# Two linear-attention blocks mixed by a gate: the gate weights issued ahead of the third chunk of key weights

## The chip, the cores and the metric

The kernel runs on one core of a Trainium2 chip. The metric is the device time of one execution in microseconds; a profiled execution also gives the span from its first to its last instruction.

## What is computed

The input `x` has 2048 rows of 640 numbers in bf16. Two linear-attention blocks A and B, of 32 heads with 20 numbers each, are applied to the same `x`, each with its own `wqkv` (640 x 1920) and `wo` (640 x 640), and a gate mixes them.

```python
def block(x, wqkv, wo):
    q, k, v = split_heads(x @ wqkv)                 # 32 heads of 20
    phi = lambda t: where(t > 0, t + 1, exp(t)) + 1e-6
    pq, pk = phi(q), phi(k)
    kv = einsum("bhsd,bhse->bhde", pk, v)
    z = einsum("bhsd->bhd", pk)
    o = einsum("bhqd,bhde->bhqe", pq, kv) / (einsum("bhqd,bhd->bhq", pq, z)[..., None] + 1e-6)
    return merge_heads(o) @ wo
g = sigmoid((x * gate_w).sum(-1, keepdims=True))
out = g * block(x, A_wqkv, A_wo) + (1 - g) * block(x, B_wqkv, B_wo)
```

The gate's sum costs no pass of its own: `gate_w` becomes one extra column (column 640) of B's key weights, so that the key matmuls of block B also give `x * gate_w` summed over each row.

## The kernel before

**Stages.** The rows of `x` are cut into 16 tiles of 128, and the 640 columns into five chunks of 128 (the contraction of the key and query matmuls). The stages on TensorE are: a few warm-up matmuls; the keys of all tiles for A and B (L660 and L661, and L825 where tiles are paired), with their phi on ScalarE and VectorE; the sums that stand for `kv` and `z` (L1186); the queries (L1058, L1154); products of weights (L1342, L1374, L1448); and the output matmuls (L1584), whose results are stored tile by tile.

**The planner.** Every operation is given to `op` or `dma` with an engine, an estimated cost, the buffers that it reads and writes, and other operations that it must follow (`after`). `Sched.run` then places operations one after the other at the earliest planned time of each engine. TensorE keeps the order in which its operations were given. The other engines take, of what could start, the operation with the earliest start, and among equals the one with the lowest `prio`, which is the order of giving unless stated otherwise. Between two operations of different engines the planner adds `HOP`, 60 ns. A load is planned with 450 ns of issue, 1500 ns of latency and its bytes at a given rate on one shared bus. `Sched.emit` writes the instructions in planned order, with a semaphore wait for each dependence that isn't known already.

**The first loads.** While the list `loading` isn't empty, `dma` chains the loads of one queue by `o.behind`, so that they are issued in the order in which they are given. ScalarE's queue gets three loads, L529 to L531: tile 1 of `x`; chunk 2 of A's key weights, through `ld_wk` with a planned size of 1280 bytes; and `gate_w`, as five rows of 128 numbers, into `GWZ`. SP's queue gets tile 0 of `x`, chunks 0, 1, 3 and 4 of A's key weights, the five chunks of B's, the transposing loads of later tiles (`xt_dma`), and the rest.

**What else ScalarE has at the start.** The operation `table` (L486) loads the table of activation functions and runs one small activation; its `prio` is 10**6, and it needs the constant `EPSC` that GpSimd sets (L484).

**What GpSimd does at the start.** It sets constants, clears `GWZ` (L502, the operation `zgw`), makes the identity `IDN` (L494), and sets a few pad columns. The load of the gate weights names `zgw` in `after`, since it fills five rows of a tile that must be zero elsewhere.

**What TensorE does at the start.** After the warm-up (L587), `x_tp` turns tiles 0 and 1 by matmuls with `IDN` (L600). VectorE copies tile 0, and ScalarE tile 1, into `XT` (L617). Then come the keys of A for both tiles, chunk by chunk. `gate_col` stands between chunk 3 and chunk 4: it turns `GWZ` by one matmul (L637), and VectorE copies the five columns into B's key weights (L640). The keys of B follow:

```python
    for c in range(4):
        for t in range(2):
            k_step("A", t, c, pss[t])
    gate_col()
    for c in range(4, NC):
        for t in range(2):
            k_step("A", t, c, pss[t])
```

Each `k_step` is a pair of matmuls, of 512 columns (L660) and of 128 (L661; 129 in block B with the gate's column). It waits for its chunk of key weights and for its part of `XT`.

Of the kernel before, what the change touches and what calls it, by code (L numbers as in the profile page):

```python
# [6 lines left out]
ACT = mybir.ActivationFunctionType  # L7
# [8 lines left out]
NC = 5  # L16
# [97 lines left out]
class Sched:  # L114
# [9 lines left out]
    def op(self, eng, fn, cost, ins=(), outs=(), after=(), prio=None, name="", dma=None):  # L124
        if eng == "ACT" and dma is None:
            after = list(after) + self.consts
        o = Op(eng, fn, cost, list(ins), list(outs), after, (self.base or len(self.ops)) if prio is None else prio, name, dma)
        self.ops.append(o)
        return o
# [184 lines left out]
def body(nc, A_x, A_wqkv, A_wo, B_x, B_wqkv, B_wo, gate_w, out, log=None):  # L314
# [24 lines left out]
    GWZ = sb("GWZ", [128, 128], bf)  # L339
# [105 lines left out]
    def dma(q, name, dst, src, nbytes, ins=(), outs=(), after=(), issue=450.0, transpose=False, prio=None, rate=330.0):  # L445
        timing = (rate, 1500.0 if loading else 1700.0) if not transpose else (140.0, 1500.0) if loading else (400.0, 1950.0)

        def fn(e):
            d = dst() if callable(dst) else dst
            with nc.allow_non_contiguous_dma(reason="layout"):  # L450
                return e.dma_start(d, src() if callable(src) else src, transpose=transpose)

        o = op(q, fn, 0.0, ins, outs, after, prio=prio, name=name, dma=(issue, nbytes) + timing)
        if loading:
            o.behind = chain.get(q)
            chain[q] = o
        return o
# [28 lines left out]
    def table(e):  # L486
# [12 lines left out]
        outs=[bid],  # L499
        name="idn",  # L500
    )
    zgw = op("POOL", lambda e: e.memset(GWZ[:, :], 0.0), 200.0, name="zgw")  # L502
# [4 lines left out]
    def ld_x(q, t):  # L507
        dma(q, "x%d" % t, XN[:, t, 0:D], x[128 * t : 128 * t + 128, :], 163840, outs=[bxn[t]])

    def ld_wk(q, X, c, size=163840):  # L510
        dma(q, "wk%s%d" % (X, c), WK[X][:, c, 0:D], wqkv[X][128 * c : 128 * c + 128, D : 2 * D], size, outs=[bwk[X, c]])
# [15 lines left out]

    bgw = Buf("gw5")
    ld_x("ACT", 1)  # L529
    ld_wk("ACT", "A", 2, 1280)  # L530
    dma("ACT", "gw", GWZ[0:NC, :], gate_w.rearrange("(c p) -> c p", p=128), 1280, outs=[bgw], after=[zgw])  # L531
    for c in range(NC):
        if c == 0:
            ld_x("SP", c)
# [1205 lines left out]
def bass_gated_mix__linear_attn_block__linear_attn_block__prompt_kernel(nc, *args):  # L1740
    body(nc, *args)
# [28 lines left out]
```

## Time and profile before

| What | us |
|---|---|
| Median of three runs | 174.75 |
| Lowest and highest of them | 174.69, 175.47 |
| The profiled execution | 174.98 |
| Its span | 173.6 |
| TensorE's matmuls busy | 171.0 |
| VectorE busy | 142.7 |
| ScalarE busy | 115.9 |

In the profile, PE is TensorE's matmuls, PEld its weight loads, DVE is VectorE, ACT is ScalarE, POOL is GpSimd and SP is SyncE. ACTq and SPq are the queues on which ScalarE and SP issue DMAs; an entry there is the time of the issue, not of the transfer. The brackets behind an entry give the idle time of the engine before it and what is taken to have ended that. Where a wait was for several things, the one named may have been done long before, and another, often a DMA, was the last. L451 is the line in `dma` that issues every load and store.

### The profile page before, as it was taken

To read this page: it belongs to the slowest core of one execution; us is meant where nothing else is said; L and a number is where in the kernel's file an instruction comes from. 1 tells how busy PE (TensorE), PEld (TensorE's weight loads), DVE (VectorE), ACT (ScalarE), POOL (GpSimd) and SP (SyncE) were. 2 spreads that over 40 slices of the span, in tenths; PEclk is the share of its full clock that TensorE was granted. 3 is DMA by queue.
4 is the path that set the end of the run, shared out by engine and by line. 5 is a ranking of instruction groups with operands and counts; after the bars stand their busy time and mean duration, and the time that the engine had idled before them with its cause. 6 is when DMAs were issued, how large, how long until landed. Compare 5 with 4: busy or idle time off the path is not lost.

```text
span 173.6 us, 3381 instructions
## 1 busy us (share of the span) xinstructions
PE 171.0 (99%) x1327; PEld 107.4 (62%) x1327; DVE 142.7 (82%) x262; ACT 115.9 (67%) x225; POOL 4.9 (3%) x17
## 2 busy tenths in 40 slices
PE   9999999999999999999999999999999999999995
PEld 4555555555577776666555565655556677777773
DVE  2277999999999946958889989799999993999541
ACT  5379999999953323235998895767799773556423
POOL 2000000000000070000000000000000000000000
DMA  7969999990000025339920003276860012370035
GB/s 231 296 133 116 230 369 365 358 180 7 4 0 0 0 42 99 75 66 184 230 58 0 4 2 73 66 203 160 261 182 17 0 38 79 82 230 4 0 112 190
DMA packets 33035, 20.59 MB, mean 119 GB/s; under 512 B 18260, under 2 KB 32892, under 8 KB 33020
## 3 DMA queue, kind: packets, MB, share of 16 engines
q1 hardware_dynamic: 31918, 19.59, 44.5%
q10 hardware_dynamic: 1102, 0.80, 1.6%
q8 instruction: 10, 0.16, 0.4%
q14 instruction: 5, 0.04, 0.1%
HBM read 10.88 MB, written 4.26 MB: 87 GB/s over the span
## 4 chain that ended last, share of the span: by engine, by line
PE 99%; ACT 0%; issue 0%; DVE 0%
PE ps L1186 22%; PE ps L1584 22%; PE ps L660 15%; PE ps L1058 14%; PE ps L1154 10%; PE ps L825 6%; PE ps L661 4%; PE ps L587 1%; PE ps L1448 1%; PE ps L1374 1%; PE ps L1342 1%; PE ps L600 1%; ACT PKS L1649 0%; DVE ONE L483 0%; PE ps L637 0%
## 5 line engine op out<-in xcount | busy, mean ns | idle before, releaser
L660 PE MATMUL ps<-WKW,XT 128*128 128x512 bf16 x120 | 34.0, 382 | 0.0
L661 PE MATMUL ps<-WKW,XT 128*128 128x128 bf16 (+1 forms) x120 | 26.4, 220 | 0.0
L1186 PE MATMUL ps<-TX,PKS 128*128 128x321 bf16 (+1 forms) x160 | 23.5, 300 | 0.0
L708 ACT ACTIVATE EKT<-ps 128x640 bf16<-128x640 f32 x30 | 20.8, 722 | 2.9 <-PE ps L661 2.5
L660 PEld LDWEIGHTS ps<-WKW,XT 128*128 128x128 bf16 x120 | 11.8, 98 | 14.5 <-DVE XT L617 0.5
L1186 PEld LDWEIGHTS ps<-TX,PKS 128*128 128x128 bf16 x160 | 15.6, 98 | 6.9 <-DVE DEN L1235 0.2
L1186 PE MATMUL ps<-XN,PKS 128*128 128x321 bf16 (+1 forms) x120 | 18.2, 300 | 0.0
L1186 PEld LDWEIGHTS ps<-XN,PKS 128*128 128x128 bf16 x120 | 11.7, 98 | 5.2
L897 DVE TENSOR_TENSOR PKS<-PKS 128x1280 bf16<-128x1280 bf16 (+2 forms) x20 | 13.0, 686 | 0.0
L720 ACT ACTIVATE PKS<-ps 128x640 bf16<-128x640 f32 x18 | 12.8, 724 | 0.0
L1216 ACT ACTIVATE EKT<-ps 128x321 f32<-128x321 f32 (+1 forms) x12 | 5.2, 438 | 11.2 <-PE ps L1186 5.6
L661 PEld LDWEIGHTS ps<-WKW,XT 128*128 128x128 bf16 x120 | 11.8, 98 | 0.0
L1090 ACT ACTIVATE EQ<-ps 128x512 bf16<-128x512 f32 x18 | 10.7, 604 | 1.5 <-PE ps L1058 1.0
L1165 ACT ACTIVATE EQ<-ps 128x1024 bf16<-128x1024 f32 x8 | 8.2, 1028 | 4.8 <-PE ps L1154 3.7
L711 DVE TENSOR_SCALAR EKT<-EKT 128x1280 bf16<-128x1280 bf16 (+1 forms) x20 | 8.3, 421 | 2.7 <-ACT EKT L708 2.7
L1058 PE MATMUL ps<-XT,WQA 128*128 128x512 bf16 x36 | 10.2, 379 | 0.0
L1067 ACT ACTIVATE PKS<-ps 128x512 f32<-128x512 f32 x12 | 7.0, 602 | 4.1 <-PE ps L1058 4.1
L1154 PE MATMUL ps<-XT,WQB 128*128 128x512 bf16 x40 | 9.4, 381 | 0.0
L1154 PE MATMUL ps<-XT,WQA 128*128 128x512 bf16 x40 | 9.3, 380 | 0.0
L1221 DVE TENSOR_TENSOR WKW<-ps,EKT 128x320 bf16<-128x320 f32 x12 | 5.8, 487 | 3.1 <-PE ps L1186 3.0
L726 DVE TENSOR_TENSOR PKS<-PKS,EKT 128x1280 bf16<-128x1280 bf16 x9 | 7.4, 820 | 0.1
L1607 DVE TENSOR_TENSOR PKS<-ps,EKT 128x320 bf16<-128x320 f32 x7 | 3.4, 492 | 4.7 <-PE ps L1584 2.2
(182 smaller groups left out, 339.3 us busy)
## 6 DMA issues: line engine op xcount, KB each, us to landing
out_dram<-PKS SPq DMA_DIRECT2D x15, 160.0 KB, 1.8
XN<-in_A_x_dram SPq DMA_DIRECT2D x1, 2240.0 KB, 9.3
WKW<-in_B_wqkv_dram SPq DMA_DIRECT2D x5, 160.0 KB, 3.7
WQA<-in_A_wqkv_dram SPq DMA_DIRECT2D x1, 800.0 KB, 10.9
WQB<-in_B_wqkv_dram SPq DMA_DIRECT2D x1, 800.0 KB, 12.1
WVA<-in_A_wqkv_dram SPq DMA_DIRECT2D x1, 800.0 KB, 11.9
PKS<-in_B_wqkv_dram SPq DMA_DIRECT2D x1, 800.0 KB, 5.1
PKS<-wpsA SPq DMA_DIRECT2D x1, 800.0 KB, 5.5
```

What stands on the lines that cost most here:

```text
L660: e.matmul(a[:, 0:512], l, WK[X][:, c, 0:512], start=(c == 0), stop=(c == NC - 1))
L661: return e.matmul(a[:, 512:w], l, WK[X][:, c, 512:w], start=(c == 0), stop=(c == NC - 1))
L708: op("ACT", lambda e, i=i, ps=ps: e.activation(evg(i), psg(ps), ACT.Exp), act_cost(D), ins=[ps] + first, outs=[ek, b], name="ke")
L711: lambda e: e.tensor_scalar(EK[:, ek.slot : ek.slot + n, :], EK[:, ek.slot : ek.slot + n, :], 1.0, EPS, op0=ALU.min, op1=ALU.add),
L720: op("ACT", lambda e, X=X, ps=ps: e.activation(pkt(X, t), psg(ps), ACT.Relu), act_cost(D), ins=[ps], outs=[rk], name="kr")
L825: r = e.matmul(a[:, lo:hi], l, m[:, lo:hi], start=(first and i == 0), stop=(i == len(prs) - 1), skip_group_check=not first)
L897: lambda e: e.tensor_tensor(out=out, in0=a, in1=b, op=ALU.subtract),
L1058: r = e.matmul(PS[:, ps.slot, :], w, x, start=(first and i == 0), stop=(i == len(prs) - 1), skip_group_check=not first)
L1090: o = [op("ACT", lambda e: e.activation(EQ[:, eq.slot + h, :], pv(), ACT.Exp), act_cost(512), ins=ins, outs=[eq, ex], name="qe")]
L1154: r = e.matmul(PS[:, ps.slot + h, :], WQ[X][:, c, g::5], XT[:, c, 1024 + 512 * h : 1536 + 512 * h], start=(c == 0), stop=(c == NC - 1))
L1186: r = e.matmul(PS[:, ps.slot, 0:w], reg[:, j, :], mov(j, w), start=(first and j == 0), stop=(j == 7), skip_group_check=not first)
L1584: r = e.matmul(PS[:, ps.slot, 0:HALF], reg(g), mov(g), start=(first and g == 0), stop=(g == NC - 1), skip_group_check=not first)
```

## The change

The load of the gate weights is given to ScalarE's queue ahead of chunk 2 of A's key weights, and no longer behind it. Nothing else in the file changes. Since the queue's loads are chained in the order of giving, chunk 2 is then issued behind the gate weights, and behind their wait for `zgw`.

```diff
@@ -527,8 +527,8 @@
 
     bgw = Buf("gw5")
     ld_x("ACT", 1)
+    dma("ACT", "gw", GWZ[0:NC, :], gate_w.rearrange("(c p) -> c p", p=128), 1280, outs=[bgw], after=[zgw])
     ld_wk("ACT", "A", 2, 1280)
-    dma("ACT", "gw", GWZ[0:NC, :], gate_w.rearrange("(c p) -> c p", p=128), 1280, outs=[bgw], after=[zgw])
     for c in range(NC):
         if c == 0:
             ld_x("SP", c)
```

## The prediction

> **What bounds the kernel now.** I read the page first, then the chain, then the first 7 us engine by engine, since the change touches only two DMA issues at the start. The page:
>
> ```profile
> span 173.6 us, 3381 instructions
> ...
> PE 171.0 (99%) x1327; PEld 107.4 (62%) x1327; DVE 142.7 (82%) x262; ACT 115.9 (67%) x225; POOL 4.9 (3%) x17
> ...
> PE 99%; ACT 0%; issue 0%; DVE 0%
> ```
>
> TensorE is busy from 0.3 us to the last stores, and the chain that ended last is PE work for 99%. So the only ways for this change to reach the end are a stall, or the closing of a hole, in TensorE's first stream. ScalarE's own order of time, from the timeline (start, duration, instruction):
>
> ```profile
> 0.12 0.40 ACTq L451 DMA_DIRECT2D XN<-in_A_x_dram  x1
> 0.56 0.44 ACTq L451 DMA_DIRECT2D WKW<-in_A_wqkv_dram  x1
> 1.04 0.57 ACTq L451 DMA_DIRECT2D GWZ<-in_gate_w_dram  x1
> 1.64 1.28 ACT L487 ACT_TABLE_LOAD   x1 [1.64 <-POOL XN L505]
> 2.94 0.20 ACT L488 ACTIVATE SCR<-EPSC 128x1 f32<-128x1 f32 x1
> 3.51 0.87 ACT L617 ACTIVATE XT<-ps 128x128 bf16<-128x128 f32 x3 [0.38 <-PE ps L600]
> ```
>
> The second and third line are the two that trade places. GWZ must be cleared before its DMA is issued (after=[zgw]); GpSimd does that here:
>
> ```profile
> 0.46 0.20 POOL L502 MEMSET GWZ<- 128x128 bf16 x1
> 0.69 0.29 POOL L494 TENSOR_SCALAR_AFFINE_SELECT IDN<-ONE 128x128 bf16<-128x128 bf16 x1
> ```
>
> The users are on PE's weight loads, from its timeline:
>
> ```profile
> 2.55 1.09 PEld L600 LDWEIGHTS ps<-IDN,XN 128*128 128x128 bf16 x10 [0.41 <-issue]
> 3.88 0.10 PEld L660 LDWEIGHTS ps<-WKW,XT 128*128 128x128 bf16 x1 [0.24 <-DVE XT L617]
> ...
> 5.25 0.10 PEld L660 LDWEIGHTS ps<-WKW,XT 128*128 128x128 bf16 x1
> ...
> 6.33 0.10 PEld L637 LDWEIGHTS ps<-IDN,GWZ 128*128 128x128 bf16 x1
> ```
>
> Counting the L660/L661 pairs (chunk by chunk, two tiles each), 3.88 is the first use of key chunk 0, 4.70 of chunk 1, 5.25 of chunk 2 (the load that moves), 5.79 of chunk 3, and 6.33 is the gate weights' only use. From 4.70 on, PE goes from pair to pair every 0.27 us with no idle entry: chunk 2 is not waited for now.
>
> When do loads land? One load at a time (time from issue to landing), first chunk 2 on ScalarE's queue, then chunk 3 on SP's:
>
> ```profile
> L451 ACTq DMA_DIRECT2D WKW<-in_A_wqkv_dram x1: 443/443/443, 0.6 to 0.6; - x1
> ...
> DMA to landing us min/median/max: 3.4/3.4/3.4
> ```
>
> ```profile
> L451 SPq DMA_DIRECT2D WKW<-in_A_wqkv_dram x1: 432/432/432, 1.4 to 1.4; - x1
> ...
> DMA to landing us min/median/max: 3.8/3.8/3.8
> ```
>
> So chunk 2 lands at 0.56 + 3.4 = 4.0, 1.25 us before its use. Read the same way, chunk 0 (issued 0.45) takes 3.3 and lands at 3.8, chunk 1 (0.91) takes 3.5 and lands at 4.4, chunk 3 (1.37) lands at 5.2.
>
> **The change, part by part.** No instruction is added or removed.
>
> *The order.* `ld_x`, `gw` and `ld_wk` are chained on ScalarE by `behind`. The planner starts them at 300 and then every 450 ns; its clear of GWZ ends at 600, plus 60 for the hop is 660, before 750. So the gate load fits behind the x load, and the table load (prio 10**6) stays behind both. Both DMAs carry 1280 bytes in the plan, so the planned bus time of every other load, and with it the order of everything later, stays. I expect the same program with two issues exchanged; SP's and GpSimd's queues are not passed.
>
> *The new wait.* ScalarE is free for the gate issue at 0.56; GWZ's clear ends at 0.46 + 0.20 = 0.66. From a release to the released instruction the nearest row is ONE's memset, over at 0.20, and the first PE load at 0.30: 0.1 us. It can't be below nothing. So the gate issue starts between 0.66 and 0.76, I take 0.72, runs 0.57, and chunk 2 is issued at 0.72 + 0.57 + 0.04 = 1.33: 0.77 later. Queued behind on ScalarE: the table load at 1.33 + 0.44 + 0.03 = 1.80 instead of 1.64, its activation over at 3.30 instead of 3.14. The next instruction, the copy at 3.51, waits for PE's transposes, so 0.21 us of cover remains and the 0.16 costs nothing. Without that cover it would cost those 0.16 us, since tile 1's first key matmul waits for that copy.
>
> *Chunk 2's landing.* Its issue-to-landing time is bounded by the rows of the same stretch: 2.4 (the first x tile, on quiet engines) to 3.8 (chunks 3 and 4). I take its own 3.4, with the same queue and one load ahead. It lands at 1.33 + 3.4 = 4.7; bounds 3.7 to 5.1. Against its use at 5.25, with 0.1 us for the hop, that leaves 0.4 us; at the upper bound nothing is left and nothing lost. Price of the move: 0.
>
> *Chunk 0's landing.* It could gain. In front of 3.88 PEld idled 0.24 us. The entry names a DVE copy, but DVE's three copies of tile 0 start at 2.98 and the first is long over, whereas chunk 0 lands at 3.8: this is the DMA's wait. And the queues at that time (q1 is SP's, q10 ScalarE's; packets, MB, share of 16 engines), from 2.50 to 2.63 and from 2.63 to 3.10 us:
>
> ```profile
> q1 hardware_dynamic: 37, 0.05, 99.0%
> ```
>
> ```profile
> q10 hardware_dynamic: 97, 0.12, 73.0%
> q1 hardware_dynamic: 49, 0.04, 27.4%
> ```
>
> Chunk 2 takes three quarters of the engines just when chunk 0's last packets are due. Issued 0.77 later, it can leave chunk 0 the engines, and the first key matmul can move up by 0 (if chunk 2's packets arrive when they did) to 0.24 us (if the hole closes). The first three 128x512 matmuls there take 583, 471 and 379 ns, so work moved forward falls in a slow stretch and is worth about half: I take 0.1 us. Chunks 1 and 3 lose nothing: no more bytes stand ahead of them than before, and each has 0.3 us or more.
>
> The Trainium skill ("TensorE: Matmul & The Clock Gate", Part 1) says that the array runs at half rate until it has been busy for about 3.4 us. By that rule the full hole would be worth 0.12 us and not 0.24; the shrinking durations agree, though the profile's granted clock reads 1.00 throughout.
>
> *The gate weights* land earlier, but PE, in order, comes to them at 6.33 with no idle entry: nothing.
>
> *Sum:* 0 + 0 - 0.1 = -0.1 us. The profiled execution took 174.98 us (span 173.6 and 1.4 around it), which gives 174.9; the median of the three runs is 0.23 lower, 174.75, so I forecast 174.7.
>
> **The rivals.**
>
> *Chunk 2 comes to hang on GpSimd* (slower). Before, no key weights depended on another engine; now chunk 2 waits for GWZ's clear. If in other executions GpSimd starts later than here by d, chunk 2 lands at 4.7 + d to 5.1 + d, and PE stalls by what goes beyond 5.15. It decides from d = 0.05 to 0.45 us on; for 0.87 us lost (0.5%) d must be 0.9 to 1.3. At d = 1 the time is 175.3 to 175.7. For it: engines start unevenly, GpSimd's first instruction is 0.29 us behind SP's. Against it: the profiled execution is only 0.23 us above the median, and GpSimd has done five other memsets before this and is still early.
>
> The Trainium skill ("DMA: Bandwidth & Descriptors", Issuing engines are not separate DMA queues) says that DMAs of both issuing engines end on the same 16 engines and interleave. By it the later chunk 2 would queue with SP's loads as chunk 3 does, which is the upper bound above, 5.1 and no stall; the shares of q1 and q10, which sum to 100%, agree.
>
> *The planner puts the table load ahead* (slower; the change then does more than it says). Table and activation take 1.28 + 0.20 + 0.04 = 1.5 us. If they were placed in front of chunk 2, it would be issued at 2.85, land at 6.3 to 6.7, and PE would stall 1.1 to 1.5 us: 175.9 to 176.3. It decides if the gate load's planned start passes 750; I work out 660.
>
> *Nothing at all.* Chunk 2's packets come when they did, because q10 is still busy with the x load (it lands at 0.12 + 2.7 = 2.8): 174.75.
>
> **How the numbers follow.** Forecast with the hole partly closed 0.60; nothing at all 0.22; GpSimd's clear late 0.14; table ahead 0.04. The first two both lie within 0.5% (0.87 us, about what a measurement of this kernel can tell from no change). Of the third some 0.04 lies beyond, and all of the fourth. The three runs of before spread over 0.45%, which puts about 0.04 of the rest beyond the line on either side. Slower 0.04 + 0.04 + 0.04 = 0.12, faster 0.04, same 0.84. The range takes the closed hole and the spread below, 174.75 - 0.24 - 0.4 = 174.1, and the rival at d = 1 above, 175.7.
>
> **What would show it.** In the changed profile ScalarE issues x, gate, chunk 2 at about 0.12, 0.72, 1.33, and the table load starts near 1.80. The copies at L617 on ScalarE still wait for PE. Chunk 2 lands near 4.7, and PEld's fifth L660 load has no idle entry. The idle time before the first L660 load shrinks from 0.24. I am wrong if PEld shows idle time before the fifth L660 load (chunk 2 late), if the table load stands ahead of chunk 2, or if the time differs while the first 7 us of PE do not.

## The result and the profile after

| | before | after |
|---|---|---|
| Median of 22 runs each, us | 175.11 | 175.94 |
| Lowest to highest | 174.59 to 175.84 | 175.66 to 177.78 |
| Span of the profiled execution | 173.6 | 174.6 |

The ratio after to before is 1.0047, 95% interval 1.0033 to 1.0062. The change costs 0.8 us. The forecast, 174.7 within 174.1 to 175.7, missed it. The two profiled executions, at 174.98 and 176.05 us, lie 1.07 us apart, a little more than the medians.

The page of the changed kernel, the lines that answer to those of before:

```profile
span 174.6 us, 3381 instructions
...
PE 171.2 (98%) x1327; PEld 107.4 (61%) x1327; DVE 142.6 (82%) x262; ACT 116.0 (66%) x225; POOL 4.9 (3%) x17
...
PE 95%; DMA 3%; SPq 0%; ACT 0%; issue 0%
```

The chain that ended last is no longer TensorE alone: 3% of it is a DMA, and its list of lines names `WKW<-in_A_wqkv_dram`, a chunk of A's key weights. ScalarE's timeline shows the two issues exchanged, and the table load behind them moved by no more than 0.04 us:

```profile
0.13 0.38 ACTq L451 DMA_DIRECT2D XN<-in_A_x_dram  x1
0.70 0.53 ACTq L451 DMA_DIRECT2D GWZ<-in_gate_w_dram  x1
1.26 0.39 ACTq L451 DMA_DIRECT2D WKW<-in_A_wqkv_dram  x1
1.68 1.28 ACT L487 ACT_TABLE_LOAD   x1 [1.68 <-POOL XN L505]
```

TensorE's weight loads, from the timeline (start, duration, instruction, idle time before it):

```profile
3.71 0.15 PEld L660 LDWEIGHTS ps<-WKW,XT 128*128 128x128 bf16 x1
...
4.24 0.15 PEld L660 LDWEIGHTS ps<-WKW,XT 128*128 128x128 bf16 x1 [0.28 <-DVE XT L617]
...
5.83 0.10 PEld L660 LDWEIGHTS ps<-WKW,XT 128*128 128x128 bf16 x1 [1.33 <-DMA WKW<-in_A_wqkv_dram]
...
6.33 0.10 PEld L660 LDWEIGHTS ps<-WKW,XT 128*128 128x128 bf16 x1
...
7.42 0.10 PEld L637 LDWEIGHTS ps<-IDN,GWZ 128*128 128x128 bf16 x1
```

Before, the first pair of chunk 1 stood here:

```profile
4.70 0.10 PEld L660 LDWEIGHTS ps<-WKW,XT 128*128 128x128 bf16 x1 [0.16 <-issue]
```

Chunk 0 is used at 3.71 with no idle entry (3.88 and 0.24 before). Then TensorE waits 1.33 us, and not for chunk 2, which was moved, but for chunk 1, the third load of this list: 5.83 against 4.70. The gate's matmul is at 7.42 against 6.33. From there on nothing differs: 174.6 - 7.42 and 173.6 - 6.33 are both about 167.2 us. So the whole loss lies before that point. SP issues chunk 1 at the same 0.92 us as before, but its landing is another, first before, then after:

```profile
L451 SPq DMA_DIRECT2D WKW<-in_A_wqkv_dram x1: 433/433/433, 0.9 to 0.9; - x1
...
DMA to landing us min/median/max: 3.5/3.5/3.5
```

```profile
L451 SPq DMA_DIRECT2D WKW<-in_A_wqkv_dram x1: 432/432/432, 0.9 to 0.9; - x1
...
DMA to landing us min/median/max: 4.9/4.9/4.9
```

It was 3.5 and is 4.9. The stretches from 3.0 us on show what the DMA engines did; in each row the last two columns are the share of 16 engines and GB/s. First the kernel before, then the changed one:

```profile
3.00:3.50 0.50, 0.50 (x8) 0.50 (x6) 0.50 (x2) 0.14 (x1) 0.00 (x0) 1.00 1.00 363
3.50:4.00 0.50, 0.49 (x5) 0.26 (x4) 0.45 (x2) 0.49 (x2) 0.00 (x0) 1.00 1.12 298
```

```profile
3.00:3.50 0.50, 0.50 (x8) 0.50 (x7) 0.40 (x2) 0.17 (x1) 0.00 (x0) 1.00 0.84 177
3.50:4.00 0.50, 0.50 (x6) 0.46 (x5) 0.50 (x2) 0.37 (x2) 0.00 (x0) 1.00 0.73 205
4.00:4.50 0.50, 0.50 (x4) 0.26 (x2) 0.06 (x1) 0.50 (x2) 0.00 (x0) 1.00 0.95 218
```

For 1.5 us the engines move about half of what they reach at their best (350 to 394 GB/s in half a us, in the runs), though they are marked 73 to 95% busy. A few packets take very long: among those of 1280 bytes that start from 2.6 to 4.5 us the median takes 55 ns in both kernels, but 16 of 317 take over 0.2 us and the longest 1.43, against 7 of 494 and 0.67 before.

A load has landed when its last part has. The trace keeps 16 landing updates for each full load. Those of chunk 1 come from 3.97 to 4.44 us before, and from 3.36 to 5.79 after. After the change nine of the 16 are in by 3.90, all ahead of the first one in the kernel before; the other seven come from 4.34 on, and the last of them ends TensorE's wait. So chunk 1 isn't late as a whole, but a part of it is.

The lag isn't made up later. SP issues one 160 KB load every 0.47 us, which is 349 GB/s, about as much as the engines move at their best, so every load behind chunk 1 keeps it. Block B's five chunks (3.7 us before, from the page's list of DMA issues):

```profile
WKW<-in_B_wqkv_dram SPq DMA_DIRECT2D x5, 160.0 KB, 4.7
```

### The profile page after: what moved, and what is told of

Its sections match the earlier page's. It is cut to its first block, busy times and chain, and to the rows that moved or that the text cites. A ratio compares the mean times of both kernels' runs of the same rounds, so it can differ in the third digit from the quotient of the medians.

```text
span 174.6 us, 3381 instructions
## 1 busy us (share of the span) xinstructions
PE 171.2 (98%) x1327; PEld 107.4 (61%) x1327; DVE 142.6 (82%) x262; ACT 116.0 (66%) x225; POOL 4.9 (3%) x17
## 4 chain that ended last, share of the span: by engine, by line
PE 95%; DMA 3%; SPq 0%; ACT 0%; issue 0%
PE ps L1186 22%; PE ps L1584 22%; PE ps L660 15%; PE ps L1058 13%; PE ps L1154 10%; PE ps L825 6%; PE ps L661 4%; DMA WKW<-in_A_wqkv_dram 3%; PE ps L1448 1%; PE ps L1374 1%; PE ps L1342 1%; SPq L451 0%; ACT PKS L1649 0%; PE ps L637 0%
```

## The experiments

Two theories first. G: the gate load's short rows, ahead of chunk 2, hold up the engines. M: chunk 2, issued 0.7 us later, meets chunks 1 and 3 and the two queues hold each other up. M was later split. L: what hurts is a load that begins late on the second queue. W: what hurts is that SP's chunk 1 begins while the second queue has nothing. In the cuts of the code below, `...` stands for what is left out; planned sizes and costs, set so that the planned order stays, are left out too.

All runs in one table. "q10" is the share of 16 engines that ScalarE's queue took from 2.6 to 2.8 us; GB/s are those of 3.0 to 3.5 and 3.5 to 4.0; "chunk" is the start of the first pair of the second chunk in use, "gate" that of the gate matmul's weight load; these are from one profiled execution each, and the last three also depend on when TensorE got faster in that execution, of which the last section tells. The ratio is against runs of the kernel before on the same chip; it is from 6 executions of e9, e10 and e11, 9 of e7, 12 of the other runs and 22 of the change.

| Run | q10 % | GB/s | chunk, us | gate, us | span, us | ratio (95%) |
|---|---|---|---|---|---|---|
| before | 33.5 | 363, 298 | 4.70 | 6.33 | 173.6 | |
| after | 7.1 | 177, 205 | 5.83 | 7.42 | 174.6 | 1.0047 (1.0033 to 1.0062) |
| e1 no gate, chunk 2 early | 32.7 | 341, 330 | 4.90 | 6.49 | 173.7 | 0.9998 (0.9980 to 1.0016) |
| e2 no gate, issue at 1.17 | 1.7 | 182, 236 | 5.28 | 7.22 | 174.3 | 1.0013 (0.9994 to 1.0032) |
| e11 no gate, issue at 1.26 | 1.7 | 159, 128 | 5.51 | 7.10 | 174.2 | 1.0005 (0.9981 to 1.0030) |
| e8 no gate, issue at 1.53 | none | 205, 200 | 4.86 | 6.59 | 173.7 | 1.0034 (1.0015 to 1.0054) |
| e3 gate in 16 rows | 7.2 | 115, 184 | 5.75 | 8.82 | 176.3 | 1.0039 (1.0016 to 1.0063) |
| e4 chunk 2 on SP | 1.7 | 289, 200 | 4.84 | 6.43 | 173.6 | 0.9994 (0.9981 to 1.0008) |
| e5 B's chunk 4 late | 4.2 | 151, 192 | 5.58 | 7.57 | 174.8 | 1.0046 (1.0023 to 1.0068) |
| e9 B's chunk 4 early | 57.8 | 325, 353 | 5.09 | 6.68 | 173.9 | 0.9996 (0.9966 to 1.0026) |
| e6 chunk 1 on ScalarE | 38.9 | 356, 369 | 4.71 | 6.34 | 173.6 | 1.0007 (0.9991 to 1.0022) |
| e7 roles exchanged | 3.7 | 169, 149 | 5.49 | 7.35 | 174.6 | 1.0038 (1.0021 to 1.0054) |
| e10 filled | 72.2 | 331, 351 | 4.75 | 6.73 | 173.9 | 1.0020 (0.9991 to 1.0049) |
| e12 spread | 49.2 | 251, 266 | 4.66 | 6.96 | 174.2 | 1.0005 (0.9988 to 1.0022) |
| e13 chunk 1 later | 10.6 | 200, 243 | 5.40 | 6.99 | 174.1 | 1.0034 (1.0014 to 1.0053) |

Span less "gate" is 167.1 to 167.5 us in every row: what these profiles differ by is decided before the gate's matmul.

The landing updates of the load that SP issues behind chunk 0 part the kernels in two groups. In before, e1, e9, e6, e10 and e12 the first of the 16 comes at 3.73 us or later, and the last 0.4 to 1.3 us behind it. In the other nine the first comes by 3.44, and the last 1.5 to 2.4 us behind it.

**e1, e2: without the gate load, chunk 2 early and late.** The cut is against the kernel before. In both, `bgw` is written by GpSimd's clear alone; in e2 chunk 2 also waits for a small memset on GpSimd (whose planned costs are lowered so that the planned order stays).

```diff
     ld_x("ACT", 1)
-    ld_wk("ACT", "A", 2, 1280)                   # e1 keeps this line
-    dma("ACT", "gw", GWZ[0:NC, :], ..., outs=[bgw], after=[zgw])
+    ld_wk("ACT", "A", 2, 1280, after=[late])     # e2
```

> The gate load is left out (the gate column is zero, so both blocks are mixed half and half), chunk 2 is issued at 0.56 us as in the kernel before. Two theories stand against each other. G: the gate load's five short rows, when they go ahead of chunk 2, hold up the engines behind them, and that made chunk 1 late. M: chunk 2's issue 0.7 us later makes its packets meet those of chunks 1 and 3, and the two queues hold each other up. M expects the time of the kernel before (175.1, within 0.2) and chunk 1 landed at 4.4. G expects the same or 0.1 to 0.2 us less, since the gate rows then hold up nobody; chunk 1 landed at 4.0 to 4.4. Either way PEld does not idle before chunk 1.

> The gate load is left out as in e1 (mixed half and half), and chunk 2 waits for a small GpSimd memset behind the others, so that it is issued at about 1.25 us, as in the changed kernel, with no gate load ahead of it. M: the stall is there in full, chunk 1 lands near 5.8, PEld idles over 1 us before chunk 1's first pair, time 175.9 (0.8 over the kernel before). G: chunk 1 lands at 4.0 to 4.4, no idle time, time 175.0 to 175.1.

e1 takes the time of before, though its profile misses both theories in one thing: chunk 1 lands at 4.86, and TensorE's weight loads wait 0.52 us for it. In e2's profile the slow stretch is there with no gate row anywhere (182 GB/s, chunk 1 landed 4.3 us after its issue), so the gate rows are not needed for it. But the times are mixed, 174.43 to 175.82, and the median of 175.47 lies between the theories, and its ratio doesn't part from 1.

**e3: the gate load in 16 rows,** in its place ahead of chunk 2 (against the changed kernel).

```diff
-    dma("ACT", "gw", GWZ[0:NC, :], gate_w.rearrange("(c p) -> c p", p=128), ...)
+    dma("ACT", "gw", EQ[0:16, 0, 0:40], gate_w.rearrange("(p f) -> p f", p=16), ...)
```

> The changed kernel with the gate load in another shape: 16 rows of 40 numbers into a scratch tile in place of 5 rows of 128 into GWZ (the gate column is then zero, so the blocks are mixed half and half); its place ahead of chunk 2 and its wait stay. M: nothing changes against the changed kernel, 175.9, chunk 1 near 5.8. G, if the rows' shortness is what counts: as slow or slower, since 16 rows of 80 bytes are shorter and touch all engines. G, if the uneven spread over 5 engines is what counts: no stall, 175.0.

Slow, so the uneven spread over five engines is not the cause. The profile fell on the slowest of the twelve executions, to which I come back at the end.

**e4: chunk 2 on SP's queue** (the cut is against the kernel before).

```diff
     ld_x("ACT", 1)
-    ld_wk("ACT", "A", 2, 1280)
     dma("ACT", "gw", ...)
     for c in range(NC):
-        if c != 2:
+        if True:
             ld_wk("SP", "A", c, ...)
```

> The gate load stays on ScalarE behind the x load, chunk 2 goes to SP's queue between chunks 1 and 3, so all key weights are on one queue and SP issues everything behind it 0.45 us later. M: no two chunks run on two queues, chunk 1 lands by 4.4, time 174.9 to 175.2. G: the gate rows at 2.6 us still hold up the engines that chunk 0 and 1 use: chunk 1 near 5.5 or later, 175.6 to 176.

The time is that of before, with the gate rows at their early place: against G as the whole cause. But the rate drops here as well (289 and 200), with one queue alone. Chunk 1 lands at 0.92 + 3.9 = 4.8, later than M expected, but still near its use. So M's wording, two queues that hold each other up, is not right either.

**e5 and e9: another tensor's load, late and early.** ScalarE takes chunk 4 of B, which nobody needs before 9 us, and A's chunk 2 goes to SP. In e5 it is issued behind the gate (1.26), in e9 ahead of it (0.55). The cut is against the kernel before.

```diff
     ld_x("ACT", 1)
+    ld_wk("ACT", "B", 4, 1280)          # e9
     dma("ACT", "gw", ...)
-    ld_wk("ACT", "A", 2, 1280)
+    ld_wk("ACT", "B", 4, 1280)          # e5
     ...
-        if c != 2:
+        if True:
             ld_wk("SP", "A", c, ...)
-    for c in range(NC):
+    for c in range(NC - 1):
         ld_wk("SP", "B", c)
```

> ScalarE issues x, gate, and then chunk 4 of B's key weights in place of A's chunk 2, which goes to SP's queue between chunks 1 and 3. So a full load is issued late on ScalarE's queue, behind the gate rows, as in the changed kernel, but from another tensor and not needed before 9 us. M in its plain form (a load that arrives on the second queue near 2.9 us holds up what runs on the first, whatever it reads): chunk 1 lands at 5.2 to 5.8, PEld idles 0.6 to 1.3 us before chunk 1's first pair, time 175.5 to 175.9. N, a narrower form (chunks 1 and 2 of one tensor read side by side are what hurts): chunk 1 lands at 4.8 or before as with everything on SP, 175.0 to 175.2.

> The pair to e5: the same loads on the same queues, but ScalarE issues chunk 4 of B second (0.56 us) and the gate third (1.04 us). Theory L: what hurts is a load that begins on the second queue late and after a pause (near 2.7 to 3.1 us). Theory W: what hurts is that SP's chunk 1 begins at 2.6 to 2.9 us on engines that have nothing from the other queue; with the other queue's load there from 2.5 on, chunk 1 begins at 3.0 to 3.2 and is not held up. Both expect no loss here: chunk 1 begins near 3.1, lands at 4.4 to 4.9, 175.0 to 175.3, some 0.4 us under e5. If it is as slow as e5 (175.6 or more), the moment of issue is not what counts, and both fall.

e5 loses what the change loses, though the late load is one that TensorE doesn't want for several us; e9 takes the time of before, although its profile has chunk 1 land at 5.05, later than expected. The same stretch in both, e5 first:

```profile
3.00:3.50 0.50, 0.50 (x8) 0.50 (x6) 0.50 (x2) 0.17 (x1) 0.00 (x0) 1.00 0.66 151
```

```profile
3.00:3.50 0.50, 0.50 (x7) 0.50 (x6) 0.49 (x2) 0.14 (x1) 0.00 (x0) 1.00 0.94 325
```

And the load on which TensorE waits for chunk 1, again e5 first:

```profile
5.58 0.10 PEld L660 LDWEIGHTS ps<-WKW,XT 128*128 128x128 bf16 x1 [1.21 <-DMA WKW<-in_A_wqkv_dram]
```

```profile
5.09 0.10 PEld L660 LDWEIGHTS ps<-WKW,XT 128*128 128x128 bf16 x1 [0.68 <-DMA WKW<-in_A_wqkv_dram]
```

So it need not be chunk 2, nor a load that TensorE waits for: e5 and e9 differ in the place of ScalarE's second full load alone, behind the gate rows and 0.7 us later, or ahead of them.

**e6 and e7: chunks 1 and 2 exchanged,** in the kernel before (e6) and, with TensorE's order as well, in the changed one (e7).

```diff
-    ld_wk("ACT", "A", 2, 1280)
+    ld_wk("ACT", "A", 1, 1280)
...
-        if c != 2:
+        if c != 1:
             ld_wk("SP", "A", c)
...
-    for c in range(4):
+    for c in (0, 2, 1, 3):              # e7 alone
```

> The kernel before with chunk 1 and chunk 2 exchanged: ScalarE issues x, chunk 1 (0.56 us), gate; SP issues chunks 0, 2, 3, 4. If M holds and what counts is how soon the load on the second queue is issued, chunk 1 lands at 4.0 to 4.2 (as chunk 2 does there now) and chunk 2 at 4.4 to 4.9, both ahead of their use, so that the stall before chunk 1, which some executions of the kernel before may have, can't occur: 174.7 to 175.1. If the order of addresses counts (chunk 1 behind or beside chunk 0 is slow, chunk 2 beside chunk 0 is not): chunk 1 lands after 4.8, time 175.2 to 175.6.

> The changed kernel with chunks 1 and 2 exchanged in every role: SP loads chunk 2 third, ScalarE loads chunk 1 behind the gate rows, and TensorE uses them in the order 0, 2, 1, 3, 4 for the first two tiles. Timing and queues are those of the changed kernel, only addresses differ. M and G: as the changed kernel, the second load on SP (now chunk 2) lands near 5.8, PEld idles 1 to 1.3 us, time 175.9. Order of addresses: no stall, 175.1.

The wait before the second chunk in use, e6 first:

```profile
4.71 0.10 PEld L660 LDWEIGHTS ps<-WKW,XT 128*128 128x128 bf16 x1 [0.21 <-issue]
```

```profile
5.49 0.10 PEld L660 LDWEIGHTS ps<-WKW,XT 128*128 128x128 bf16 x1 [1.11 <-DMA WKW<-in_A_wqkv_dram]
```

e7 is about as slow as the change. e6's median of 175.30 would fit the order of addresses, but the kernel before had 175.25 on that chip, and chunk 1 landed at 3.96, not after 4.8. So which chunk is on which queue isn't what counts. An earlier chunk 1 buys nothing over the kernel before.

**e8 and e11: the lateness alone, in other sizes.** As e2, with other memsets.

```diff
-    late = op("POOL", lambda e: e.memset(GE[:, :], 0.0), ...)
+    late = op("POOL", lambda e: e.memset(EQ[:, 0, 0:448], 0.0), ...)    # e8; 0:120 in e11
```

> As e2 (no gate load, blocks mixed half and half, chunk 2 waits for a GpSimd memset) with a longer memset, so that chunk 2 is issued near 1.6 to 1.7 us and lands near 6. M, with the hold-up growing with the lateness: chunk 1 lands at 5.2 to 6, time 175.7 to 176.3 (up to 0.1 of it from the later table load). If instead the gate rows make most of the changed kernel's loss, and e2's was the spread: chunk 1 by 4.9, chunk 2 by 5.6, 175.2 to 175.6.

> As e2 (no gate load, blocks mixed half and half) with the memset sized so that chunk 2 is issued at 1.26 us, as in the changed kernel. If the gate rows add nothing to the loss: 175.8 to 176.0, with no execution under 175.5. If they make part of it: a median of 175.3 to 175.7, with some executions near 175.0, as in e2.

e8 has a median of 175.98, but its executions run from 174.86 to 176.42, and its profile is of one of the shorter ones, in which TensorE waits 0.89 us for chunk 1 and then gets it at 4.86. e11, with chunk 2 issued at the same 1.26 us as in the change, has a median of 175.49 in six executions and an interval that ends at 1.0030, below where the change's begins (1.0033). So lateness alone is enough for the slow stretch, and at 1.53 us (e8) for a loss; at 1.17 and 1.26 (e2, e11) no loss is shown. The gate rows ahead seem to make the loss the rule: with them all 22 executions of the change took 175.66 us or more, without them some escape. But that rests on intervals that only just part, and in e13 below, which has the rows ahead, some escape too.

**e10: ScalarE's queue filled ahead of the late load.** Chunk 4 of B stands between x and the gate, so chunk 2 comes later than in the change (1.63).

```diff
     ld_x("ACT", 1)
+    ld_wk("ACT", "B", 4, 1280)
     dma("ACT", "gw", ...)
     ld_wk("ACT", "A", 2, 1280)
     ...
-    for c in range(NC):
+    for c in range(NC - 1):
         ld_wk("SP", "B", c)
```

> The changed kernel with one load more ahead of the gate on ScalarE's queue: x, chunk 4 of B (which SP then leaves to it), gate, chunk 2. The second queue is busy from 1.6 to about 3.5 us without a pause, and chunk 2 comes later still (issued near 1.8, landed near 5). W: chunk 1 begins near 3.1 and lands at 4.4 to 4.9; at most 0.3 us lost on chunk 2; 175.0 to 175.4. L: chunk 2's late beginning holds up what SP has, chunk 1 or chunk 3 lands after 5.4, 175.6 or more. The table load is about 0.4 us later and may cost up to 0.1.

```profile
3.00:3.50 0.50, 0.50 (x9) 0.42 (x6) 0.50 (x2) 0.49 (x3) 0.00 (x0) 1.00 1.01 331
3.50:4.00 0.50, 0.09 (x2) 0.00 (x0) 0.44 (x2) 0.50 (x4) 0.00 (x0) 1.00 1.06 351
```

The slow stretch is gone with the latest chunk 2 of all, so L, as put, falls: chunk 1 is used at 4.75. What is lost is lost otherwise: chunk 0 shares the engines with the filler (first key load at 4.17), and TensorE waits 0.54 us for chunk 2 itself. The median of 175.62 is 0.2 over what W expected (the kernel before had 175.44 on that chip), and the ratio parts from neither kernel.

**e12 and e13: both queues filled by other means, and chunk 1 held back.** In e12 ScalarE takes chunks 1 and 3, SP 0, 2 and 4 and then the gate. In e13, the changed kernel, SP's chunk 1 waits for a memset on GpSimd.

```diff
# e12, against before
-    ld_wk("ACT", "A", 2, 1280)
-    dma("ACT", "gw", ...)
+    ld_wk("ACT", "A", 1, 1280); ld_wk("ACT", "A", 3, 1280)
...
-        if c != 2:
+        if c not in (1, 3):
             ld_wk("SP", "A", c, ...)
+    dma("SP", "gw", ...)
# e13, against after
-            ld_wk("SP", "A", c)
+            ld_wk("SP", "A", c, after=[late] if c == 1 else ())
```

> Chunks alternate between the queues: ScalarE issues x, chunk 1, chunk 3; SP issues x, chunks 0, 2, 4, then the gate load, then B's chunks. Both queues have a load at every moment up to about 4 us. W (a load on SP's queue that begins while the other queue is empty is held up): no slow stretch before 4 us, chunk 1 lands at 4.0 to 4.3, chunks 2 and 3 by 5, PEld idles nowhere before a key chunk; 174.6 to 175.0, so at least the kernel before, and perhaps 0.2 to 0.4 us better, since chunk 1 has more in hand than there. If it is 175.3 or more, an earlier chunk 1 buys nothing.

> The changed kernel, with SP's chunk 1 and all behind it held back by a GpSimd memset until about 1.3 us (issued 0.92 before), so that chunk 1 can begin at 3.0 to 3.1 us at the earliest, at the same time as chunk 2 on the other queue; that queue is empty from about 2.7 on, as in the changed kernel. W: chunk 1 has company from its first packet and isn't held up for more than it shares: lands at 4.4 to 5.0, 175.1 to 175.5, better than the changed kernel although it is issued later. If the hold-up is there all the same (chunk 1 at 5.8 or later, 175.9 to 176.4), it is not a question of chunk 1's beginning but of both queues having run empty.

e13 goes against W as I had put it. Chunk 1 and chunk 2 are issued together, at 1.25 and 1.26, and begin together, so chunk 1 has company from its first packet, and the rate is low all the same. The outcome lies between the two that were expected: chunk 1 lands at 5.36, the median is 175.72.

```profile
3.00:3.50 0.50, 0.50 (x8) 0.50 (x6) 0.50 (x2) 0.15 (x1) 0.00 (x0) 1.00 0.81 200
```

What e13 shares with the change is told by the packet records of the trace, with each queue's packets counted off by 128 to a load in order of their start. That is rough where some packets lag. In e13 chunk 0's last packet and the first one of ScalarE's next load both start at 2.65 us.

e12's start is as in the kernels without loss, and TensorE waits there for no key chunk, but SP's own queue starts no packet from 2.89 to 3.08, and its rate of 251 and 266 GB/s lies below that of the other five kernels that have a full load on ScalarE's queue under way at 2.6 us. Chunks 2 and 3 land at 5.23 and 5.77, not by 5. It misses the gain that was expected: as fast as before, so no version beat the kernel before.

**What is settled and what stays open.** e5 against e9 and e7 against e6 show that the loss comes with the place of ScalarE's second full load, and not with which load it is. In both pairs the slow kernel has that load later and behind the gate rows at once. That the rows alone don't do it is shown by e4, and that lateness without them can is shown by e8; how much they add to the change's own loss stays open, since e11, as late as the change but without them, shows none.

What goes with the slow stretch is clearer. With that load under way at 2.6 to 2.8 us (q10 at 32% or more), the engines went on at about 300 GB/s or more until 4 us in five of six kernels, e12 the exception; without it they fell to 115 to 289 in all nine. By the packet count, ScalarE's next load starts before chunk 0's last packet does in the six (2.64 and 3.17 us in before, 2.57 and 3.02 in e9). In eight of the nine it starts together with it or after it (3.03 and 2.85 in after, 2.76 and 2.69 in e5, 2.71 and 2.68 in e2, 2.65 and 2.65 in e13); e4 has no such load. SP's queue doesn't run empty there: in all nine its next packet starts within 0.01 us of chunk 0's last. So SP's chunk behind chunk 0 begins while ScalarE's queue has nothing under way, or in e13 at the same moment, and then a part of it lands late. That is a coincidence of times in one profile of each kernel. Why single packets then take up to 1.4 us isn't settled, since no run looks inside a queue.

## Why the prediction was wrong, step by step

The order of issues was right: 0.70, 1.26 and 1.68 against 0.72, 1.33 and 1.80, the new wait ending 0.03 us behind the clear of GWZ (0.46 + 0.21) against 0.06 taken. The table load was covered as argued. The hole in front of chunk 0 closed as argued, fully: chunk 0 landed at 3.47 instead of 3.77, and its first weight load stands at 3.71 instead of 3.88 with no idle time. Of these 0.17 us, 0.05 were left at the second tile's pair (4.24 instead of 4.29), against the 0.1 taken. It was then lost in the wait for chunk 1.

The step that failed stands in one sentence: "Chunks 1 and 3 lose nothing: no more bytes stand ahead of them than before, and each has 0.3 us or more." It counted bytes and took the engines' rate as given. The rate was not given: it fell to half for 1.5 us, and the last part of chunk 1, with 0.3 us in hand, came 1.4 us later. That one term, set at 0, measured +1.1 us in the profiles (4.70 to 5.83). That the moved load brings this about is shown by the experiments; by which mechanism it does is open.

The step for chunk 2 failed the same way. Its 3.4 us, with bounds of 2.4 to 3.8, were rows of a pattern that the change broke; it took 4.9, and chunk 2 landed at 6.15. Against its old use at 5.25 that is a stall of 0.9 us, where the sum had 0. It didn't show because the wait for chunk 1 had already moved that use to 6.33: luck, and not cover. The row that could have warned was there: with both queues busy the engines ran at 353 to 376 GB/s, close to SP's 349 GB/s of issue, so a slow moment could stay in every load behind it. The bounds should have allowed for that, and one of the rivals should have been a key chunk other than the one moved coming late.

The base was off too. Of the 1.24 us between forecast and result, 0.36 is the median of three runs, 174.75, which 22 runs put at 175.11.

None of the rivals happened. GpSimd's clear was over at 0.67, 0.01 us later than forecast, and made chunk 2 no later than the forecast had it, the table load stayed behind, and the packets did not come when they had. The Trainium skill ("DMA: Bandwidth & Descriptors", Issuing engines are not separate DMA queues) was read as saying that the later load would only queue and interleave. It does share the engines, as q1 and q10 show. But in e5 and e9 the engines' rate changes with the place of that load (151 and 325 GB/s), and the upper bound of 5.1 us, at which that reading also arrived, was passed by 1 us (1.26 + 4.9).

## What to carry to other kernels

Before a load is moved in a crowded start, look at every load that runs beside it, and above all at the one with the least in hand, which here had 0.3 us and was not the one moved. Where the issue rate of one queue is about what the engines move, as here (349 GB/s against 350 to 394), a lag of 1 us stays. Here the kernels in which the second queue had a full load under way at 2.6 us showed no clear loss, so keep it so while the first consumers wait. The time from issue to landing belongs to the pattern of loads around a load, and a row from the old pattern is no bound once that pattern is changed. And a load has landed when its slowest part has: look at all its landing updates, and not at a mean rate.

## What was not expected of the hardware

The rate of TensorE at the start differs from execution to execution. In e12's profile TensorE waits for no chunk, yet the key pairs come every 0.53 us until 5.7 us, where in the kernel before they come every 0.27 us from 4.70 on:

```profile
4.66 0.15 PEld L660 LDWEIGHTS ps<-WKW,XT 128*128 128x128 bf16 x1 [0.28 <-issue]
...
5.19 0.15 PEld L660 LDWEIGHTS ps<-WKW,XT 128*128 128x128 bf16 x1 [0.28 <-issue]
...
5.72 0.15 PEld L660 LDWEIGHTS ps<-WKW,XT 128*128 128x128 bf16 x1 [0.28 <-issue]
...
6.14 0.10 PEld L660 LDWEIGHTS ps<-WKW,XT 128*128 128x128 bf16 x1 [0.17 <-issue]
```

e3's profile, behind a wait of 1.37 us for chunk 1, keeps the slow step, 0.53 us, until 8.9 us, and that execution took 177.69 us where its others took 175.5 to 176:

```profile
8.29 0.15 PEld L660 LDWEIGHTS ps<-WKW,XT 128*128 128x128 bf16 x1 [0.28 <-issue]
...
8.93 0.15 PEld L660 LDWEIGHTS ps<-WKW,XT 128*128 128x128 bf16 x1
```

The Trainium skill ("TensorE: Matmul & The Clock Gate", Part 1) has the half rate end after a busy window of about 3.4 us that runs freely and isn't tied to the kernel's start. The two profiles agree in that the moment differs; the granted clock in the profile reads 1.00 all the while. Whether a stall for a chunk makes the slow step last, and so costs more than its own length, isn't shown: in the changed kernel's own profile the pairs come every 0.23 to 0.27 us straight behind a wait of 1.33 us, and the kernel before had executions of 177.5 to 177.8 us too, one on each of three chips. The spread of the kernel before, 174.59 to 175.84, may come from the same source; that was not tried.
